# A fused attention and MLP kernel: MLP units three steps later, longer DVE sums, copies of q on ScalarE

## The chip, the cores and the metric

The kernel runs on one core of a Trainium2 chip. The metric is the device time of one execution in microseconds, as the median of several runs. PE is TensorE (PEld its weight loads), DVE is VectorE, ACT is ScalarE, POOL is GpSimd, SP is SyncE, which here only issues DMAs.

## The reference

Causal attention with a forgetting decay, for 8 batches of 8 heads, 576 positions and head dimension 64, feeds a two-layer MLP over the 4608 tokens (512 features, 2048 hidden):

```python
scores = scale * q @ k.T                       # per batch and head
cum = np.cumsum(np.log(np.clip(f, 1e-4, 1)))
scores = where(causal, -1e9, scores + cum[:, None] - cum[None, :])
attn = softmax(scores)
x = (attn @ v) rearranged to [B * S, H * D]
h = x @ w_in
g = h - np.tanh(h)
out = g @ w_out
```

The MLP needs all 8 heads of a token, so it runs behind the attention.

## The kernel before, in words

**Attention.** Heads are taken in pairs: 4 pairs per batch, 32 pairs `(b, c)` in all. `scores` (line 256) makes one of 7 tiles of a pair's transposed scores on PE (the tiles have one or two matmuls, line 266), takes the exponential on ACT (line 272) and masks on POOL (line 280). The decay is folded into three extra rows of `QT` and `KT`. `values` (line 283) multiplies with v and a column of ones (line 290), and DVE normalizes into `xn` (lines 294 to 296). `turn` (line 299) brings `xn` transposed into `XR`, a ring of four batches: for the first batch by PE, from the second by two DMA transposes on SP's queue (lines 310 and 312).

The transposed q and k come in two ways. Up to batch 2, `trans` (line 229) transposes a pair's q or k on PE into a PSUM tile, and two copies of 64 x 576 bring it to `QT` or `KT`, on DVE (line 244) or ACT (line 242). From batch 3 on, `turn_block` (line 97) does it by DMA into `TQ` and `TK`, and `place` copies on DVE (line 102). The loads of q, k and v from HBM go through POOL's queue (lines 88 to 114).

**MLP.** The 4608 tokens are 9 units of 512. `mlp1` (line 314) has 16 steps per unit: 4 matmuls of 512 columns into a PSUM tile `hps` (line 324), a tanh of -h on ACT (line 327) and an add on DVE into `gq` (line 331). `mlp2` (line 346) has 14 steps of 8 matmuls of 256 columns (line 353). It uses a Strassen-like scheme with 7 products instead of 8: `wout` is seen as 2 x 2 blocks B11 to B22, and line 205 makes the differences W1, W2, W4 and a new B12 once, 8 instructions of 128 x 1024. The unit's g is seen as blocks A11 to A22, and line 338 makes sums S1, S2 and S3 (S3 in the place of A21); line 375 makes S4 in the place of A12. `STEPS` (line 344) names the order of the products. The results are added up on DVE (`plus`, line 359; one copy on ACT, line 369) and leave by four DMAs of 256 KB per unit (line 365).

In the kernel before, `gq` holds a quarter of a unit, four steps of `mlp1`; the sums are made after every fourth step, in pieces of 512.

**The order of the work.** The order on PE, POOL, SP and DVE is the order of the program, written out by hand; on ACT a scheduler decides. The outer loop (line 424) runs over slots `p` from 0 to 32. Slot `p` holds the scores of pair `p`, the values of pair `p - 1` (behind tile 2), the transposes of pair `p + 1`, a `turn`, and the loads that `LOADS` lists for `(p, tile)`. Between these items it strews MLP steps evenly:

```python
    TAKE = (0, 0, 0, 0, 2, 8, 7, 7, 6)
            take = TAKE[p] if p < len(TAKE) else 8 - (p - len(TAKE)) % 2
```

`TAKE` gives 30 steps to slots 4 to 8, which is one unit; from slot 9 on slots take 8 and 7 by turns, 30 in four slots. So unit `u` begins with slot `4u + 5`. The last pair of batch `u`, pair `4u + 3`, has its values in slot `4u + 4`, behind tile 2, and its `turn` behind tile 3. Unit `u` reads tokens `512u` to `512u + 511`, and from unit 1 on these reach into batch `u`. What is left after slot 32 runs alone at the end (line 442): 60 steps, the last two units.

Buffers: `ps_m` has 4 PSUM tiles that `hps`, the products of `mlp2` and the tiles of `trans` share in turn; `ps_sc` has 2 for scores. `gq` has 5 buffers, `sq` (S1 and S2) 4, `th` and `ost` 2 each.

Of the kernel before, what the change touches and what calls it, by code (L numbers as in the profile page):

```python
# [21 lines left out]
def kernel(  # L22
# [10 lines left out]
    nc = tc.nc  # L33
    P = 128
# [6 lines left out]
    NPAIR = H // 2  # L41
# [5 lines left out]
    NK = NFT // 2  # L47
    HU = 256
    HE = DM // 2
    NCH = DM // P  # L50
    UW = 512
# [4 lines left out]
    wpl = ctx.enter_context(tc.tile_pool(name="wpl", bufs=1))  # L56
    aex = ctx.enter_context(tc.tile_pool(name="aex", bufs=10))
    fin = ctx.enter_context(tc.tile_pool(name="fin", bufs=3))
    gtp = ctx.enter_context(tc.tile_pool(name="gtp", bufs=5))
    tmp = ctx.enter_context(tc.tile_pool(name="tmp", bufs=2))  # L60
    acc = ctx.enter_context(tc.tile_pool(name="acc", bufs=1))
    PSUM = bass.MemoryType.PSUM
# [6 lines left out]
    W1 = wpl.tile([P, NK, HE], FP16)  # L69
    W2 = wpl.tile([P, NK, HE], FP16)  # L70
    W4 = wpl.tile([P, NK, HE], FP16)
    B11, B12 = wout[:, 0:NK, 0:HE], wout[:, 0:NK, HE:DM]
    B21, B22 = wout[:, NK:NFT, 0:HE], wout[:, NK:NFT, HE:DM]
# [114 lines left out]
    def load_wout(t0, t1):  # L188
# [3 lines left out]
    LOADS = {(0, 1): [lambda: load_qk(qn, q, 1, 0, 2), lambda: load_qk(kn, k, 1, 0, 2)],  # L192
             (0, 4): [lambda: load_qk(qn, q, 1, 2, H)],
             (1, 0): [lambda: load_qk(kn, k, 1, 2, H)],
             (1, 2): [lambda: load_win(0, DFF // 2)],
             (1, 5): [lambda: load_v_rest(1), lambda: load_v_head(1, 0)],
             (2, 1): [lambda: load_v_head(1, 1), lambda: load_win(DFF // 2, DFF)],
             (4, 0): [lambda: load_wout(0, NFT // 2)],
             (4, 2): [lambda: load_wout(NFT // 2, NFT)]}
    for n in range(NJ - 1):  # L200
        LOADS.setdefault((3, n), []).append(lambda n=n: load_v_block(1, n, 2, H))
    for n in range(2):
        ks = slice(n * NK // 2, (n + 1) * NK // 2)
        for i, (o, x, y) in enumerate(((W1, B12, B11), (B12, B22, B12), (W2, B22, W1), (W4, B21, W2))):
            LOADS.setdefault((NPAIR + 2, i), []).append(lambda o=o, x=x, y=y, ks=ks: nc.vector.tensor_tensor(
                out=o[:, ks, :], in0=x[:, ks, :], in1=y[:, ks, :], op=ALU.subtract))
    LOADS.setdefault((NPAIR, 5), []).append(lambda: load_qk(qn, q, 2, 0, H))
    LOADS.setdefault((NPAIR, 6), []).append(lambda: load_qk(kn, k, 2, 0, H))
# [18 lines left out]
    E, XN, GQ, SQ, M2 = {}, {}, {}, {}, {}  # L227
# [86 lines left out]
    def mlp1(u, s):  # L314
        pr, half = divmod(s, 2)
        ft = half * NK + pr
        hps = ps_m.tile([P, UW], FP32, tag="m", name="hps")
        t0 = u * UW % RING
        parts = [(0, t0, min(UW, RING - t0))]
        if t0 + UW > RING:  # L320
            parts.append((RING - t0, 0, t0 + UW - RING))
        for o, t, n in parts:
            for ci in range(NCH):
                nc.tensor.matmul(out=hps[:, o:o + n], lhsT=win[:, ci, ft * P:(ft + 1) * P],  # L324
                                 rhs=XR[:, ci, t:t + n], start=(ci == 0), stop=(ci == NCH - 1))
        th = tmp.tile([P, UW], FP32, tag="th", name="th")
        nc.scalar.activation(out=th, in_=hps, func=AF.Tanh, scale=-1.0)  # L327
        if s % 4 == 0:
            GQ[(u, s // 4)] = gtp.tile([P, 2, 2, UW], FP16, tag="gq", name="gq")
        gq = GQ[(u, s // 4)]  # L330
        nc.vector.tensor_tensor(out=gq[:, half, pr % 2, :], in0=hps, in1=th, op=ALU.add)  # L331
        if s % 4 == 3:
            sq = SQ[(u, s // 4)] = gtp.tile([P, 2, 2, HU], FP16, tag="sq", name="sq", bufs=4)
            a11, a21 = gq[:, 0, :, 0:HU], gq[:, 0, :, HU:UW]
            a22 = gq[:, 1, :, HU:UW]
            for o, x, y, op in ((sq[:, 0], a21, a22, ALU.add), (sq[:, 1], sq[:, 0], a11, ALU.subtract),
                                (a21, a11, a21, ALU.subtract)):
                nc.vector.tensor_tensor(out=o, in0=x, in1=y, op=op)  # L338

    LHS = {"A11": lambda u, i: GQ[(u, i)][:, 0, :, 0:HU], "A12": lambda u, i: GQ[(u, i)][:, 1, :, 0:HU],  # L340
           "A22": lambda u, i: GQ[(u, i)][:, 1, :, HU:UW], "S3": lambda u, i: GQ[(u, i)][:, 0, :, HU:UW],
           "S1": lambda u, i: SQ[(u, i)][:, 0], "S2": lambda u, i: SQ[(u, i)][:, 1]}
    LHS["S4"] = LHS["A12"]
    STEPS = [("A11", B11), ("S2", W2), ("A12", B21), ("S3", B12), ("S1", W1), ("A22", W4), ("S4", B22)]

    def mlp2(u, s):
        n, m = divmod(s, 2)
        lhs, rhs = STEPS[n]
        if m == 0:
            M2["ps"] = ps_m.tile([P, 2, HE], FP32, tag="m", name="ops")  # L350
        ps = M2["ps"]
        for kt in range(NK):
            nc.tensor.matmul(out=ps[:, m, :], lhsT=LHS[lhs](u, kt // 2)[:, kt % 2, m * P:(m + 1) * P],  # L353
                             rhs=rhs[:, kt, :], start=(kt == 0), stop=(kt == NK - 1))
        if m == 0:
            return

        def plus(src, to):
            nc.vector.tensor_tensor(out=to, in0=ps, in1=src, op=ALU.add)  # L359
            return to  # L360

        def total(src, r, e):
            ost = plus(src, tmp.tile([P, 2, HE], FP32, tag="ost", name="ost"))
            r0 = u * UW + r * HU
            nc.sync.dma_start(out=out[r0:r0 + HU, e * HE:(e + 1) * HE].rearrange("(m p) e -> p m e", p=P), in_=ost)

        if lhs == "A11":
            M2["m1"] = acc.tile([P, 2, HE], FP32, tag="m1", name="m1")
            nc.scalar.activation(out=M2["m1"], in_=ps, func=AF.Copy)
        elif lhs == "S2":  # L370
            M2["u2"] = plus(M2["m1"], acc.tile([P, 2, HE], FP32, tag="u2", name="u2"))
        elif lhs == "A12":
            total(M2["m1"], 0, 0)
            for i in range(4):
                nc.vector.tensor_tensor(out=LHS["S4"](u, i), in0=LHS["A12"](u, i), in1=LHS["S2"](u, i), op=ALU.subtract)  # L375
        elif lhs == "S3":
            M2["u3"] = plus(M2["u2"], acc.tile([P, 2, HE], FP32, tag="u3", name="u3"))
        elif lhs == "S1":
            total(M2["u3"], 1, 1)
            plus(M2["u2"], M2["u2"])  # L380
        elif lhs == "A22":
            total(M2["u3"], 1, 0)
        else:
            total(M2["u2"], 0, 1)
# [3 lines left out]
    def att_items(p):  # L388
        def put(fn, *args):
            items.append((lambda: fn(*args), True))  # L390

        items = []
        here = pairs[p] if p < len(pairs) else None
        before = pairs[p - 1] if 0 < p <= len(pairs) else None
        after = pairs[p + 1] if p + 1 < len(pairs) else None
        early = p < NPAIR
        if p == 0:
            put(trans, *here, qn, QT, "AA")
            put(trans, *here, kn, KT, "VV")
        for ti in range(len(TILES)):  # L400
            if here:
                put(scores, *here, ti)
            for load in LOADS.get((p, ti), ()):
                items.append((load, False))
            if ti == 0 and after and after[0] < FAR:
                put(trans, *after, qn, QT, "VV")
            if ti == (1 if early else 3) and after and after[0] < FAR:
                put(trans, *after, kn, KT, "VV")
            if ti == 2 and before:
                put(values, *before)  # L410
            if p < NPAIR:
                if ti == 1 and p > 1:
                    put(turn, *pairs[p - 2])
            elif p == NPAIR and ti in (1, 5):
                put(turn, *pairs[p - 2 + (ti == 5)])
            elif p > NPAIR and ti == 3:
                put(turn, *before)
        return items

    mlp = [(fn, u, s) for u in range(NU) for fn, n in ((mlp1, NFT), (mlp2, 2 * len(STEPS))) for s in range(n)]  # L420
    TAKE = (0, 0, 0, 0, 2, 8, 7, 7, 6)
    at = 0
    with tc.manual_schedule(engines={PE, mybir.EngineType.Pool, mybir.EngineType.SP, mybir.EngineType.DVE}):
        for p in range(len(pairs) + 1):
# [47 lines left out]
```

## Time and profile before

| What | us |
|---|---|
| Median of 3 runs | 394.73 |
| Lowest and highest run | 390.86, 394.89 |
| The profiled execution | 392.38 |
| Its span, first to last instruction | 390.7 |
| PE busy | 344.6 |
| DVE busy | 295.9 |
| ACT busy | 206.9 |
| POOL busy | 166.9 |

A row of the groups of instructions has the line, engine, operation, out<-in with shapes and count, then the busy time, the mean in ns, and the engine's idle time just before them with what ended it. A row of the timeline has start, length, engine, line and operation, a count where neighbours are merged, and in brackets the idle time before it and what ended it. Matmul starts are exact; their ends are modelled, so neighbours overlap. A row of the waits has the engine and line that waited, what for, the sum, how many times, and the longest. A row of the stretches has the stretch, its length, the busy time of each engine with the count, the granted TensorE clock as a share of full speed, the DMA share and GB/s.

### The profile page before, as it was taken

The numbers are of one execution on the slowest core, as the hardware profiler recorded it, in microseconds if no ns is written. First come the engines' busy times: TensorE is split into PE (matmuls) and PEld (weight loads), VectorE is DVE, ScalarE is ACT, GpSimd is POOL, SyncE is SP. The second block draws the span as 40 slices with busy tenths as digits, with TensorE's granted clock in tenths as the row PEclk, the third lists the DMA queues.
The fourth block names the chain that finished last, engine by engine and source line by source line (L and its number), as shares of the span: only waits on it lengthen the run. The fifth ranks groups of instructions, "written<-read, shape, count | busy, mean of one in ns | idle before, by whom it ended". The sixth has DMA issues, their size and how long they took to land. (4 is left out here: it accounts for less than half of the span.)

```text
span 390.7 us, 8437 instructions
## 1 busy us (share of the span) xinstructions
PE 344.6 (88%) x3156; PEld 235.0 (60%) x3156; DVE 295.9 (76%) x563; ACT 206.9 (53%) x388; POOL 166.9 (43%) x340
## 2 busy tenths in 40 slices
PE   1898977988989799969998899969999999999995
PEld 0665533864548446844587788735686577467474
DVE  7678998775999378936886588728896866876973
ACT  5588653434763478426853585427646861641620
POOL 7979622573346543754277336734222221000000
PEclk9999995998999899998999899969999999999999
DMA  8999991999939992999599969998122012103003
GB/s 102 167 183 194 207 171 18 81 142 130 108 32 100 172 142 50 92 155 147 86 69 135 175 91 64 132 151 109 33 59 82 15 30 72 55 2 107 2 1 107
DMA packets 145324, 38.79 MB, mean 99 GB/s; under 512 B 128084, under 2 KB 144196, under 8 KB 145284
## 3 DMA queue, kind: packets, MB, share of 16 engines
q0 software_dynamic: 92416, 18.37, 56.4%
q1 hardware_dynamic: 52868, 19.90, 24.5%
q8 instruction: 24, 0.39, 0.4%
q14 instruction: 16, 0.13, 0.1%
HBM read 36.85 MB, written 9.44 MB: 118 GB/s over the span
## 5 line engine op out<-in xcount | busy, mean ns | idle before, releaser
L324 PE MATMUL hps<-XR,win 128*128 128x512 f16 (+1 forms) x640 | 150.7, 373 | 21.7 <-DMA XR<-xn 16.6
L272 ACT ACTIVATE e<-ps 128x512 f16<-128x512 f32 x192 | 110.8, 598 | 51.4 <-PE ps L266 49.1
L327 ACT ACTIVATE th<-hps 128x512 f32<-128x512 f32 x144 | 86.1, 599 | 85.3 <-PE hps L324 67.3
L331 DVE TENSOR_TENSOR gq<-hps,th 128x512 f16<-128x512 f32 x144 | 96.1, 687 | 44.7 <-ACT th L327 42.2
L280 POOL TENSOR_SCALAR_AFFINE_SELECT e<-e 128x128 f16<-128x128 f16 (+1 forms) x192 | 68.3, 360 | 111.6 <-ACT e L272 109.1
L324 PEld LDWEIGHTS <-win 128*128 128x128 f16 x640 | 60.7, 101 | 60.7 <-issue 14.1
L266 PE MATMUL ps<-QT,KT 67*128 67x64 f16 (+4 forms) x384 | 81.6, 295 | 9.2 <-DMA KT<-clo 3.3
L353 PEld LDWEIGHTS <-gq 128*128 128x128 f16 x720 | 68.3, 98 | 18.2 <-DVE gq L331 4.3
L353 PE MATMUL ops<-wout,gq 128*128 128x256 f16 x576 | 75.1, 276 | 3.8 <-DVE gq L331 3.7
L266 PEld LDWEIGHTS <-KT 67*128 67x128 f16 x384 | 38.0, 103 | 48.7 <-issue 23.9
L290 PEld LDWEIGHTS <-e 128*128 128x128 f16 x896 | 34.6, 101 | 4.5 <-issue 0.8
L290 PE MATMUL av<-vn,e 128*128 128x65 f16 x896 | 35.7, 197 | 0.6 <-POOL e L280 0.6
L353 PE MATMUL ops<-W,sq 128*128 128x256 f16 x288 | 36.1, 273 | 0.0
L359 DVE TENSOR_TENSOR ost<-ops,u 128x512 f32<-128x512 f32 x27 | 18.6, 690 | 22.1 <-DMA out_dram<-ost 12.5
L113 POOL DMA_DIRECT2D vn<-in_v_dram x32 | 27.9, 874 | 3.6 <-issue 3.0
L353 PEld LDWEIGHTS <-sq 128*128 128x128 f16 x288 | 26.9, 98 | 3.8
L296 DVE TENSOR_TENSOR xn<-av,rs 128x640 f16<-128x640 f32 x32 | 26.4, 825 | 1.1
L280 POOL TENSOR_SCALAR_AFFINE_SELECT el<-el 128x128 f16<-128x128 f16 x32 | 9.8, 306 | 33.7 <-ACT el L272 33.7
L244 DVE COPY QT<-t 64x576 f16<-64x576 f16 x22 | 17.6, 802 | 7.5 <-PE t L235 7.4
L94 POOL DMA_DIRECT2D kn<-in_k_dram x25 | 21.2, 848 | 2.3 <-issue 2.3
L94 POOL DMA_DIRECT2D qn<-in_q_dram x25 | 21.2, 847 | 2.1 <-issue 1.8
L272 ACT ACTIVATE el<-ps 128x128 f16<-128x128 f32 x32 | 8.8, 275 | 24.3 <-PE ps L266 24.2
(58 smaller groups left out, 248.2 us busy)
## 6 DMA issues: line engine op xcount, KB each, us to landing
out_dram<-ost SPq DMA_DIRECT2D x36, 256.0 KB
vn<-in_v_dram POOLq DMA_DIRECT2D x24, 128.0 KB, 4.4
qn<-in_q_dram POOLq DMA_DIRECT2D x20, 128.0 KB, 3.6
kn<-in_k_dram POOLq DMA_DIRECT2D x20, 128.0 KB, 5.0
win<-in_moe_w_in_dram POOLq DMA_DIRECT2D x2, 1024.0 KB, 11.5
wout<-in_moe_w_out_dram POOLq DMA_DIRECT2D x2, 1024.0 KB, 12.0
XR<-xn SPq DMA_TRANSPOSE x56
vn<-in_v_dram POOLq DMA_DIRECT2D x12, 64.0 KB, 4.1
```

Of the source, the lines that this page charges most:

```text
L94: nc.gpsimd.dma_start(out=dst[b % 2][0:pn, n, :].rearrange("p (h d) -> p h d", h=H), in_=src[b, :, n * P:n * P + pn, :].rearrange("h p d - ...
L113: nc.gpsimd.dma_start(out=vn[b % 2][:, n, h0:h1, 0:D], in_=v[b, h0:h1, n * P:(n + 1) * P, :].rearrange("h p d -> p h d"))
L266: nc.tensor.matmul(out=ps[:, col:col + n], lhsT=KT[b % 2][:, h, j * P:(j + 1) * P], rhs=QT[b % 2][:, h, i0:i0 + n])
L272: nc.scalar.activation(out=e[:, lo:hi], in_=ps[:, lo:hi], func=AF.Exp, scale=qscale)
L280: nc.gpsimd.affine_select(out=view, in_=view, compare_op=ALU.is_ge, fill=0.0, base=0, pattern=pat, channel_multiplier=-1)
L290: nc.tensor.matmul(out=av[:, a, ib, :], lhsT=E.pop((b, c, a, j, ib)), rhs=vn[b % 2][:, j, 2 * c + a, 0:D + 1], start=(j == 0), stop=(j == ib))
L296: nc.vector.tensor_tensor(out=xn.rearrange("p i (a d) -> p a i d", a=2), in0=av[:, :, :, 0:D], in1=rs.to_broadcast([P, 2, NJ, D]), op=ALU. ...
L324: nc.tensor.matmul(out=hps[:, o:o + n], lhsT=win[:, ci, ft * P:(ft + 1) * P], rhs=XR[:, ci, t:t + n], start=(ci == 0), stop=(ci == NCH - 1))
L327: nc.scalar.activation(out=th, in_=hps, func=AF.Tanh, scale=-1.0)
L331: nc.vector.tensor_tensor(out=gq[:, half, pr % 2, :], in0=hps, in1=th, op=ALU.add)
L353: nc.tensor.matmul(out=ps[:, m, :], lhsT=LHS[lhs](u, kt // 2)[:, kt % 2, m * P:(m + 1) * P], rhs=rhs[:, kt, :], start=(kt == 0), stop=(kt ...
L359: nc.vector.tensor_tensor(out=to, in0=ps, in1=src, op=ALU.add)
```

## The change

- `TAKE` gives 2, 7, 6, 6 and 6 steps to slots 4 to 8, 27 instead of 30. Every unit now begins three steps into slot `4u + 5`, and 63 steps are left after slot 32.
- `gq` and `sq` hold half a unit (8 steps); the sums are made after every eighth step in pieces of 1024, and so is S4. Both have 2 buffers. The SBUF that they take goes from 28 to 24 KB per partition.
- The eight weight differences move from slot 6 to slots 5 (W1 behind tiles 3 and 4, B12 behind tiles 5 and 6) and 6 (W2 behind tiles 1 and 2, W4 behind tiles 4 and 5).
- In `STEPS` the product of A12 comes second and that of S2 third.
- The copies of the transposed q are on ACT for slots 4 to 10; those of k stay on DVE.
- `ost` has 3 buffers instead of 2.

```diff
-    gtp = ctx.enter_context(tc.tile_pool(name="gtp", bufs=5))
+    gtp = ctx.enter_context(tc.tile_pool(name="gtp", bufs=2))
...
-            LOADS.setdefault((NPAIR + 2, i), []).append(lambda o=o, x=x, y=y, ks=ks: nc.vector.tensor_tensor(
+            LOADS.setdefault((NPAIR + 1 + i // 2, (3, 5, 1, 4)[i] + n), []).append(lambda o=o, x=x, y=y, ks=ks: nc.vector.tensor_tensor(
                 out=o[:, ks, :], in0=x[:, ks, :], in1=y[:, ks, :], op=ALU.subtract))
...
-        if s % 4 == 0:
-            GQ[(u, s // 4)] = gtp.tile([P, 2, 2, UW], FP16, tag="gq", name="gq")
-        gq = GQ[(u, s // 4)]
-        nc.vector.tensor_tensor(out=gq[:, half, pr % 2, :], in0=hps, in1=th, op=ALU.add)
-        if s % 4 == 3:
-            sq = SQ[(u, s // 4)] = gtp.tile([P, 2, 2, HU], FP16, tag="sq", name="sq", bufs=4)
+        if s % 8 == 0:
+            GQ[(u, s // 8)] = gtp.tile([P, 2, NK // 2, UW], FP16, tag="gq", name="gq")
+        gq = GQ[(u, s // 8)]
+        nc.vector.tensor_tensor(out=gq[:, half, pr % 4, :], in0=hps, in1=th, op=ALU.add)
+        if s % 8 == 7:
+            sq = SQ[(u, s // 8)] = gtp.tile([P, 2, NK // 2, HU], FP16, tag="sq", name="sq")
...
-    STEPS = [("A11", B11), ("S2", W2), ("A12", B21), ("S3", B12), ("S1", W1), ("A22", W4), ("S4", B22)]
+    STEPS = [("A11", B11), ("A12", B21), ("S2", W2), ("S3", B12), ("S1", W1), ("A22", W4), ("S4", B22)]
...
-            ost = plus(src, tmp.tile([P, 2, HE], FP32, tag="ost", name="ost"))
+            ost = plus(src, tmp.tile([P, 2, HE], FP32, tag="ost", name="ost", bufs=3))
...
-            for i in range(4):
+            for i in range(2):
                 nc.vector.tensor_tensor(out=LHS["S4"](u, i), in0=LHS["A12"](u, i), in1=LHS["S2"](u, i), op=ALU.subtract)
...
-                put(trans, *after, qn, QT, "VV")
+                put(trans, *after, qn, QT, "VV" if early else "AA")
...
-    TAKE = (0, 0, 0, 0, 2, 8, 7, 7, 6)
+    TAKE = (0, 0, 0, 0, 2, 7, 6, 6, 6)
```

The reads in `mlp2` change their indices with the halves (`kt // 4`, `kt % 4`).

More of the change, by code (lines that the diff above doesn't have):

```diff
@@ L327, in mlp1 @@
         nc.scalar.activation(out=th, in_=hps, func=AF.Tanh, scale=-1.0)
-        if s % 4 == 0:
-            GQ[(u, s // 4)] = gtp.tile([P, 2, 2, UW], FP16, tag="gq", name="gq")
-        gq = GQ[(u, s // 4)]
-        nc.vector.tensor_tensor(out=gq[:, half, pr % 2, :], in0=hps, in1=th, op=ALU.add)
-        if s % 4 == 3:
-            sq = SQ[(u, s // 4)] = gtp.tile([P, 2, 2, HU], FP16, tag="sq", name="sq", bufs=4)
-            a11, a21 = gq[:, 0, :, 0:HU], gq[:, 0, :, HU:UW]
-            a22 = gq[:, 1, :, HU:UW]
+        if s % 8 == 0:
[4 more added lines that the diff above has]
+            sq = SQ[(u, s // 8)] = gtp.tile([P, 2, NK // 2, HU], FP16, tag="sq", name="sq")
+            a11, a21, a22 = gq[:, 0, :, 0:HU], gq[:, 0, :, HU:UW], gq[:, 1, :, HU:UW]
             for o, x, y, op in ((sq[:, 0], a21, a22, ALU.add), (sq[:, 1], sq[:, 0], a11, ALU.subtract),
@@ L352, in mlp2 @@
         for kt in range(NK):
-            nc.tensor.matmul(out=ps[:, m, :], lhsT=LHS[lhs](u, kt // 2)[:, kt % 2, m * P:(m + 1) * P],
+            nc.tensor.matmul(out=ps[:, m, :], lhsT=LHS[lhs](u, kt // 4)[:, kt % 4, m * P:(m + 1) * P],
                              rhs=rhs[:, kt, :], start=(kt == 0), stop=(kt == NK - 1))
```

## The prediction, made before the changed kernel ran

> **What bounds the kernel now.** I read the page first, then the waits of PE, then a table of stretches cut at the slots' first score matmuls, then the timeline around the long waits. A "slot" is one pass of the loop over `p`.
>
> ```profile
> span 390.7 us, 8437 instructions
> PE 344.6 (88%) x3156; PEld 235.0 (60%) x3156; DVE 295.9 (76%) x563; ACT 206.9 (53%) x388; POOL 166.9 (43%) x340
> ```
> ```profile
> PE hps L324 <- DMA XR<-xn: 16.6, 5, 4.1
> PE hps L324 <- DVE gq L331: 5.0, 8, 2.0
> ```
>
> PE is busy 88% of the span. Its largest wait is 16.6 us in five pieces, for the transposes that bring an attention output into XR. In the stretches below the columns are length, then busy time of PE, PEld, DVE, ACT and POOL, then the granted TensorE clock, DMA share and GB/s.
>
> ```profile
> 37.89:48.73 10.84, 10.07 (x88) 5.45 (x86) 9.83 (x18) 7.58 (x15) 7.17 (x12) 1.00 1.26 207
> 48.73:66.38 17.65, 12.07 (x88) 6.23 (x87) 17.19 (x31) 7.29 (x14) 3.53 (x8) 0.80 0.99 105
> 76.89:85.01 8.12, 8.12 (x104) 6.88 (x102) 7.43 (x13) 3.53 (x7) 6.42 (x14) 1.00 1.23 144
> 85.01:100.69 15.68, 11.79 (x88) 5.98 (x87) 9.39 (x17) 7.57 (x15) 7.02 (x14) 0.89 1.29 139
> 100.69:112.38 11.69, 9.49 (x82) 5.12 (x83) 11.05 (x21) 7.76 (x15) 3.22 (x9) 1.00 0.41 70
> 130.35:144.32 13.97, 11.20 (x76) 5.41 (x75) 7.37 (x14) 7.44 (x15) 6.51 (x12) 0.88 1.48 156
> 170.63:185.71 15.08, 11.20 (x76) 5.43 (x75) 7.36 (x14) 7.43 (x15) 6.38 (x12) 0.89 1.41 148
> 212.03:226.31 14.28, 11.26 (x108) 8.84 (x107) 7.36 (x14) 7.43 (x15) 6.75 (x13) 0.88 1.52 167
> 252.66:269.53 16.87, 12.54 (x76) 6.31 (x75) 7.56 (x14) 7.43 (x15) 6.37 (x12) 0.80 1.27 134
> 295.84:305.48 9.64, 9.37 (x76) 4.91 (x75) 7.35 (x14) 7.37 (x15) 2.13 (x7) 1.00 0.26 74
> ```
>
> Rows one to four are slots 5, 6, 8 and 9. Row five is slot 10. The last five are slots 13, 17, 21, 25 and 29, which hold the same PE work: the start of a new MLP unit. Slot 29 takes 9.64 us at full clock without a wait; the other four take 4.33, 5.44, 4.64 and 7.23 us more. The timeline says why, and the clock says that a wait costs twice.
>
> ```profile
> 133.87 0.38 PE L324 MATMUL hps<-XR,win 128*128 128x512 f16 x1 [2.49 <-DMA XR<-xn]
> 215.97 0.27 PE L324 MATMUL hps<-XR,win 128*128 128x256 f16 x1 [2.80 <-DMA XR<-xn]
> 257.75 0.59 PE L324 MATMUL hps<-XR,win 128*128 128x512 f16 x1 [4.06 <-DMA XR<-xn]
> ```
> ```profile
> 59.30:69.50 10.20, 8.05 (x35) 4.37 (x35) 8.34 (x16) 3.85 (x7) 2.93 (x5) 0.50 0.08 16
> 90.00:93.40 3.40, 3.40 (x16) 1.52 (x14) 2.65 (x4) 1.68 (x3) 0.03 (x1) 0.50 0.94 146
> 134.40:137.80 3.40, 3.40 (x12) 1.36 (x10) 1.38 (x2) 2.05 (x4) 1.58 (x3) 0.51 1.53 135
> 216.30:219.70 3.40, 3.40 (x18) 2.36 (x17) 1.38 (x2) 2.15 (x4) 1.46 (x3) 0.50 1.80 138
> 257.20:264.00 6.80, 6.25 (x42) 3.44 (x42) 2.08 (x3) 2.77 (x5) 2.46 (x4) 0.50 1.23 182
> ```
>
> After each of the five waits PE runs at half clock: four times for 3.4 us (three of the four are shown, two of them after the waits of 2.49 and 2.80) and once for 6.8 us. Half of that time is lost: (4 x 3.4 + 6.8) / 2 = 10.2 us. So the five waits cost 16.6 + 10.2 = 26.8 us. A sixth half-clock stretch, 10.2 us from 59.3, follows waits for DVE in slot 6.
>
> **Unit starts, three steps later.** Nothing is added; three MLP steps now stand ahead of the old place, with the attention work that lies between steps. How much PE time that is can be read in slot 29, where nothing waits: the first step starts at 296.06, the fourth at 300.00.
>
> ```profile
> 296.06 1.03 PE L324 MATMUL hps<-XR,win 128*128 128x512 f16 x4
> ...
> 300.00 1.03 PE L324 MATMUL hps<-XR,win 128*128 128x512 f16 x4
> ```
>
> The cover is 3.94 us. The waits run from 2.49 (unit 2) to 4.06 (unit 5), so at most 0.12 us stays, in unit 5, provided that XR lands when it does now. What sets the landing: the two transposes leave SP as soon as xn is written, and DVE writes xn after the values.
>
> ```profile
> 249.56 0.38 SPq L365 DMA_DIRECT2D out_dram<-ost  x1
> 250.84 1.23 SPq L310 DMA_TRANSPOSE XR<-xn  x1
> 252.14 1.22 SPq L312 DMA_TRANSPOSE XR<-xn  x1
> ```
>
> Landing comes 257.75 - 250.84 = 6.9 us after the first issue. In the changed order the output DMA at 249.56 comes behind these two on SP, and the four small sums of line 375 that DVE did just ahead of this xn fall in the slot before. Both can only bring XR forward. The two outputs that end a unit now follow the five transposes into TQ on SP; a third `ost` buffer keeps DVE from waiting for them. POOL keeps its order. I take 26.7 us of gain; the bounds are 0 (XR moves along with the unit) and 26.8.
>
> The Trainium skill, "TensorE: Matmul & The Clock Gate", section "HAM oscillation — how this bites in real kernels", gives an abstract rule of "no PE-idle gaps >~3.4µs". By it the waits of 2.49 and 2.80 would not have halved the clock, the clock's part would be (2 x 3.4 + 6.8) / 2 = 6.8 instead of 10.2, and my sum would end 3.4 us higher. The trace does not agree: the rows at 134.40 and 216.30 show half clock after shorter waits, so I give that no chance here.
>
> **DVE: sums in pieces of 1024, copies moved, differences spread.**
>
> ```profile
> L338 DVE TENSOR_TENSOR gq<-gq 128x512 f16<-128x512 f16 x36 | 16.9, 471 | 0.0
> L338 DVE TENSOR_TENSOR sq<-gq 128x512 f16<-128x512 f16 x36 | 15.6, 433 | 1.2
> L338 DVE TENSOR_TENSOR sq<-sq,gq 128x512 f16<-128x512 f16 x36 | 15.5, 430 | 1.2
> L244 DVE COPY QT<-t 64x576 f16<-64x576 f16 x22 | 17.6, 802 | 7.5 <-PE t L235 7.4
> ```
> ```profile
> L205 DVE TENSOR_TENSOR W<-wout x2: 681/684/686, 52.6 to 53.2; 128x1024 f16<-128x1024 f16 x2
> ```
> ```profile
> L242 ACT ACTIVATE QT<-t x2: 796/800/805, 7.2 to 8.0; 64x576 f16<-64x576 f16 x2
> ```
>
> Before: 108 sums of 512, 48.0 us. After: 54 of 1024, at the 0.684 us of line 205, 36.9 us. So 11.1 us less on DVE, but a burst is 2.05 us instead of 1.3. The q copies of seven slots (4 to 10) leave DVE, 2 x 0.80 us each, and load ACT by as much. All of this counts only where DVE is late.
>
> That is slots 5 and 6 first: DVE is busy 9.83 + 17.19 = 27.0 of 28.5 us. From it go two pairs of q copies (3.2), one gq (14 steps become 13, 0.7), and three bursts of 1.3 become one of 2.05 (1.9). The eight differences stay in these two slots. 21.2 us are left. PE needs 10.07 - 0.87 = 9.2 and 8.12 (slot 8's length, six steps and no wait), 17.3 us, so DVE still sets these slots, at 21.2. Slots 7 and 8 hold six steps each, 2 x 8.12. With one half-clock stretch of 3.4 us (1.7; the bounds are none and today's 5.1) it makes 39.1 instead of 85.01 - 37.89 = 47.1: 8.0 us of gain. Of this 2.6 us (3 x 0.87) is work that comes back at the end, where slot 32 leaves 63 steps instead of 60.
>
> The new place of the differences adds a wait. They read wout, whose halves must have landed.
>
> ```profile
> L189 POOL DMA_DIRECT2D wout<-in_moe_w_out_dram x2: 883/887/891, 33.7 to 35.2; - x2
> DMA to landing us min/median/max: 10.2/12.0/13.9
> ```
>
> The halves land at 33.7 + 10.2 = 43.9 and 35.2 + 13.9 = 49.1 at the latest. The first difference stands behind six gq (at about 43 to 44), the first that reads the second half behind nine gq, two KT copies and the first burst (at about 49 to 50). I take 0; if DVE came 2 us sooner it would hold gq, KT copies and xn behind it, and PE through the PSUM buffers, for 2 us.
>
> Slot 10 waited for DVE too:
>
> ```profile
> 107.14 1.89 PE L324 MATMUL hps<-XR,win 128*128 128x512 f16 x8 [0.31 <-DVE gq L331]
> 112.38 0.39 PE L266 MATMUL ps<-QT,KT 67*128 67x512 f16 x1 [1.62 <-DVE KT L244]
> ```
>
> With 1.6 us of q copies off DVE these 1.9 us go. What is late next there is ACT: 7.76 + 1.6 = 9.4 of a slot of 9.8 us. The copies' cost on ACT lies between 0 and 7 x 1.6 = 11.2 us; ACT has 3 us or more to spare in each of these slots today, so I take 0.5 in all.
>
> **The larger bursts elsewhere.** A burst holds gq, and so PSUM buffers, 0.75 us longer. Fourteen bursts lie in the slots, so the bounds are 0 and 10.5 us. PE waited 5.0 us for gq in the whole run, so I take 1.5, mainly in slots 11, 15, 19, 23 and 27, where the place copies now stand among the last gq.
>
> **The tail.** Two units run there alone, and DVE sets the pace of their first halves:
>
> ```profile
> 341.23 2.69 DVE L331 TENSOR_TENSOR gq<-hps,th 128x512 f16<-128x512 f32 x4
> 345.09 2.69 DVE L331 TENSOR_TENSOR gq<-hps,th 128x512 f16<-128x512 f32 x4
> ```
>
> Four steps take 3.86 us there against 3.47 on PE. Now the first eight go at PE's 0.87, then the burst, then seven gq at 0.67 until A11 can end: 1.7 + 7 x 0.87 + 0.7 + 2.05 + 4.7 = 15.2 us against 15.9. I take 0.7 per unit, 1.4 in all. A12 before S2 gives DVE the 1.7 us of A12 to finish its sums, so S2 does not wait.
>
> **The sum.** -26.7 (XR and its clock) - 8.0 (slots 5 to 8) - 1.9 (slot 10) + 2.6 (three steps at the end) - 1.4 (tail) + 1.5 (bursts) + 0.5 (ACT) = -33.4. The profiled execution took 392.38 us, 1.7 more than its span; that gives 359.0. The median of the runs, 394.73, lies 2.35 above that execution; I leave that to the range.
>
> **Rivals.**
> One: XR lands later as well. Today POOL sends the slot's second load of v only when the wait is over, since its selects follow the scores; with PE running on, one or two 128 KB loads go out while the transposes are under way. If that delays them by 2 us, 16.6 + 5 x 2 - 5 x 3.94 = 6.9 us of waits stay, and if the clock falls as today, 10.2 more: about 376. The Trainium skill, "DMA: Bandwidth & Descriptors", section "Queues, rings and completion order", speaks for it: each DMA engine takes turns between the queues that have work. Against it: most of the 6.9 us passes before the second load could go.
> Two: the first units gain nothing but their three steps, because DVE meets wout too early or the clock stays low: 8.0 - 2.6 = 5.4 more, 364.4. DVE is the bound there in either case, which speaks for it.
> Three, the other side: the 2.05 us bursts find DVE so late that all PSUM buffers are full, and PE stands for the burst and then runs at half clock. Fourteen times (2.05 + 1.7) is 52 us, which outweighs 33.4: about 411. It decides from about 9 of the 14 on. Against it: DVE is busy 7.4 of 9.64 us in a slot without waits.
>
> **How the numbers follow.** My forecast has 0.68, rival one 0.14, rival two 0.13, rival three 0.03, no change for a reason that I don't see 0.02. The range reaches from 351 (no half clock early, no new waits, XR early) to 370, past rival two and half-way to rival one, and leaves out 0.2. About 1% is what a measurement of this kernel can tell from no change. Faster 0.95, within 1% 0.02, slower 0.03.
>
> **What would show it.** In the new profile the waits for XR should be under 1 us in sum, with PEclk at 1.00 from slot 9 on; slots 13, 17, 21, 25 should take 9.6 to 10 us; the sums should be 54 of about 0.68 us; slot 9 should start near 77. It is wrong if XR waits remain with half clock behind them, if waits for gq exceed some 8 us, or if DVE shows a wait for wout.

## The result and the profile after

The changed kernel takes 370.6 us, the median of four runs (369.06 to 373.72); the kernel before, in four runs beside it, takes 393.7. The ratio is 0.943, with a 95% interval of 0.935 to 0.952: faster by 23.1 us, where 33.4 had been forecast, and 0.6 us above the upper end of the predicted range. The profiled execution took 373.72 us, 3.1 above the median. Ratios here and below leave out the runs that came out slower than the others of the same kernel, medians do not: of the four runs of e8 one, of 369.30 us, is such a run, and the median of the other three is 364.5.

The page of the changed kernel, its span and busy times, and then its longest waits of PE that are not the start of the program:

```profile
span 371.6 us, 8348 instructions
PE 337.5 (91%) x3156; PEld 232.4 (63%) x3156; DVE 280.7 (76%) x477; ACT 215.6 (58%) x402; POOL 164.8 (44%) x340
```
```profile
PE ops L352 <- DVE gq L331: 7.0, 10, 1.0
...
PE hps L324 <- DVE gq L331: 3.9, 4, 2.5
```

No wait for XR is left. At the top now stands a wait of `ops`, the first product of `mlp2`, for `gq`: ten times, 0.7 us on average, all in slots 11, 15, 19, 23 and 27. The kernel before had this wait too, but its six lay in slot 6 and behind the last slot:

```profile
PE ops L353 <- DVE gq L331: 3.7, 6, 1.9
```

The stretches, cut at the first score matmul of slots 5, 6, 9, 10, 13 and 15 (columns as in the prediction):

```profile
42.42:52.59 10.17, 9.33 (x84) 5.00 (x82) 6.61 (x12) 8.65 (x16) 6.41 (x12) 1.00 1.25 200
52.59:64.86 12.27, 8.62 (x78) 4.60 (x79) 12.09 (x21) 8.91 (x17) 3.41 (x10) 1.00 1.65 110
82.75:92.53 9.78, 9.78 (x101) 6.58 (x98) 6.62 (x12) 7.43 (x13) 6.51 (x13) 1.00 2.23 161
92.53:105.29 12.76, 10.13 (x84) 5.34 (x82) 9.46 (x16) 8.56 (x16) 3.02 (x9) 0.92 0.87 133
125.12:134.38 9.26, 9.26 (x89) 6.06 (x88) 5.34 (x10) 5.87 (x12) 6.29 (x12) 1.00 1.82 148
142.71:154.48 11.77, 9.90 (x93) 6.28 (x91) 10.93 (x20) 6.96 (x14) 6.51 (x13) 1.00 0.93 86
```

And slot 15 of the kernel before, which the prediction did not show:

```profile
152.68:162.23 9.55, 9.43 (x105) 7.62 (x102) 8.47 (x17) 5.22 (x10) 6.60 (x12) 1.00 0.89 58
```

Read the two slots 15 together. PE's work goes from 9.43 to 9.90, but the slot from 9.55 to 11.77, and DVE is busy 10.93 of it. It is the same in slots 11, 19, 23 and 27. Laid side by side, the two profiles give this account of the change in time, against the terms of the prediction's sum (lengths in us, from the starts of the slots' first score matmuls):

| Stretch | Before | After | Change | Forecast |
|---|---|---|---|---|
| up to slot 4 | 31.3 | 33.8 | +2.5 | 0 |
| slot 4 | 6.55 | 8.62 | +2.1 | part of the +0.5 for ACT |
| slots 5 to 8 | 47.1 | 40.3 | -6.8 | -8.0 |
| slot 9 | 15.7 | 9.8 | -5.9 | with the next |
| slots 13, 17, 21, 25 | 60.2 | 37.1 | -23.1 | -26.7 with slot 9 |
| slot 10 | 11.7 | 12.8 | +1.1 | -1.9, and part of the +0.5 for ACT |
| slots 11, 15, 19, 23, 27 | 47.7 | 57.5 | +9.8 | +1.5 |
| slot 29 to the end | 94.8 | 96.4 | +1.6 | +2.6 - 1.4 |

From slot 5 on the sum is 352.8 before and 329.2 after, 23.6 less (the slots that the table leaves out change by 0.1 in sum), which is near what the medians show.

The first line is not the change's. Slot 4 begins between 29.8 and 34.1 us in the fourteen traced kernels, and two of the experiments (e4, e11), which are the same program as the kernel before up to slot 5, begin it at 33.6 and 33.2. What differs is the pace of PE in the slots ahead of it. The changed kernel and e3, from 20 us to the start of slot 4:

```profile
20.00:33.80 13.80, 12.90 (x124) 8.93 (x122) 10.25 (x18) 10.09 (x20) 10.53 (x24) 1.00 1.23 189
20.00:29.88 9.88, 8.38 (x122) 5.95 (x122) 8.94 (x16) 9.27 (x20) 9.23 (x21) 1.00 1.27 183
```

124 matmuls are busy for 12.90 us in the one and 122 for 8.38 us in the other. The clock column says 1.00 for both, so it does not show this.

The second line is the change's, in these two profiles. In slot 4 the copies of q on ACT stand ahead of exponentials that PE needs, and half clock follows (slot 4 of the kernel before, then a matmul and a stretch in slot 4 of the changed kernel):

```profile
31.34:37.89 6.55, 5.87 (x73) 3.70 (x72) 5.35 (x10) 5.60 (x11) 6.25 (x15) 1.00 1.63 189
```
```profile
37.07 0.22 PE L266 MATMUL ps<-QT,KT 67*128 67x64 f16 x2 [0.86 <-ACT e L272]
```
```profile
38.40:41.80 3.40, 3.40 (x16) 1.77 (x15) 0.89 (x2) 2.35 (x5) 2.54 (x6) 0.51 1.21 171
```

With these copies on DVE slot 4 takes 6.55 us in the kernel before and 6.29 in e4 and e11; with the copies on ACT it takes 7.74 to 8.63 in the eight traced kernels that have them there. Other things lengthen this slot too: e3, e8 and e9, with the copies on DVE, take 7.74 to 8.97 us, e3 and e9 with a wait for `win` of 0.8 and 1.4 us, e8 with slow matmuls. In what follows the profiled executions are compared from slot 5 on.

What bounds slot 15 is seen in its order on DVE, and in the two matmuls that wait (first DVE, then PE):

```profile
147.24 0.67 DVE L331 TENSOR_TENSOR gq<-hps,th 128x512 f16<-128x512 f32 x1
147.94 1.43 DVE L102 COPY QT<-TQ 64x1152 f16<-64x1152 f16 x2
149.41 0.69 DVE L331 TENSOR_TENSOR gq<-hps,th 128x512 f16<-128x512 f32 x1
150.01 1.19 DVE L102 COPY KT<-TK 64x1152 f16<-64x1152 f16 x2
...
151.56 0.82 DVE L296 TENSOR_TENSOR xn<-av,rs 128x640 f16<-128x640 f32 x1
152.30 0.68 DVE L331 TENSOR_TENSOR gq<-hps,th 128x512 f16<-128x512 f32 x1
153.02 0.69 DVE L337 TENSOR_TENSOR sq<-gq 128x1024 f16<-128x1024 f16 x1
```
```profile
150.15 1.16 PE L352 MATMUL ops<-wout,gq 128*128 128x256 f16 x9 [0.98 <-DVE gq L331]
...
153.04 0.28 PE L352 MATMUL ops<-wout,gq 128*128 128x256 f16 x1 [0.75 <-DVE gq L331]
```

DVE has no pause here. The unit's last `gq` instructions stand between place copies and an `xn`, and the product of A11 reads them as soon as they are there, at 150.15 and 153.04. In the kernel before, the unit's last `gq` of this slot is ahead of the short burst and of all place copies (DVE in slot 15):

```profile
155.01 0.69 DVE L331 TENSOR_TENSOR gq<-hps,th 128x512 f16<-128x512 f32 x1 [0.78 <-ACT th L327]
...
157.09 2.26 DVE L102 COPY QT<-TQ 64x1152 f16<-64x1152 f16 x4
```

### The profile page after: what moved, and what is told of

It reads as the page before. It is cut to its first block, busy times and chain, and to the rows that moved or that the text cites. A ratio compares the mean times of both kernels' runs of the same rounds, so it can differ in the third digit from the quotient of the medians.

```text
span 371.6 us, 8348 instructions
## 1 busy us (share of the span) xinstructions
PE 337.5 (91%) x3156; PEld 232.4 (63%) x3156; DVE 280.7 (76%) x477; ACT 215.6 (58%) x402; POOL 164.8 (44%) x340
## 3 DMA queue, kind: packets, MB, share of 16 engines
q1 hardware_dynamic: 52868, 19.90, 26.7%
## 4 chain that ended last, share of the span: by engine, by line
PE 55%; DVE 25%; ACT 9%; issue 6%; DMA 3%; POOL 1%; POOLq 0%; DVEq 0%; SPq 0%; ACTq 0%
PE ops L352 26%; PE hps L324 13%; PE ps L266 9%; DVE gq L331 8%; ACT e L272 4%; PE av L290 4%; ACT th L327 4%; DVE QT L102 3%; DVE sq L337 3%; DVE xn L296 3%; DVE KT L244 2%; PE t L235 2%; DMA XR<-xn 2%; DVE KT L102 1%; DVE gq L337 1%
## 5 line engine op out<-in xcount | busy, mean ns | idle before, releaser
L324 PE MATMUL hps<-XR,win 128*128 128x512 f16 (+1 forms) x640 | 144.0, 362 | 5.1 <-DVE gq L331 3.9
L327 ACT ACTIVATE th<-hps 128x512 f32<-128x512 f32 x144 | 87.0, 606 | 66.1 <-PE hps L324 54.4
L331 DVE TENSOR_TENSOR gq<-hps,th 128x512 f16<-128x512 f32 x144 | 97.7, 688 | 34.2 <-ACT th L327 32.7
L280 POOL TENSOR_SCALAR_AFFINE_SELECT e<-e 128x128 f16<-128x128 f16 (+1 forms) x192 | 67.0, 352 | 100.8 <-ACT e L272 98.9
L324 PEld LDWEIGHTS <-win 128*128 128x128 f16 x640 | 58.6, 98 | 55.9 <-issue 10.2
L266 PE MATMUL ps<-QT,KT 67*128 67x64 f16 (+4 forms) x384 | 80.0, 295 | 11.5 <-DMA KT<-clo 4.6
L358 DVE TENSOR_TENSOR ost<-ops,u 128x512 f32<-128x512 f32 x27 | 18.7, 691 | 28.1 <-PE ops L352 28.0
L352 PEld LDWEIGHTS <-sq 128*128 128x128 f16 x288 | 27.1, 97 | 4.8
L94 POOL DMA_DIRECT2D qn<-in_q_dram x25 | 21.2, 846 | 2.6 <-issue 2.6
L244 DVE COPY KT<-t 64x576 f16<-64x576 f16 x24 | 19.1, 797 | 0.3
L352 PE MATMUL ops<-W,gq 128*128 128x256 f16 x144 | 18.2, 272 | 0.0
```

The source lines that it names most:

```text
L94: nc.gpsimd.dma_start(out=dst[b % 2][0:pn, n, :].rearrange("p (h d) -> p h d", h=H), in_=src[b, :, n * P:n * P + pn, :].rearrange("h p d - ...
L244: nc.vector.tensor_copy(out=to, in_=of)
L266: nc.tensor.matmul(out=ps[:, col:col + n], lhsT=KT[b % 2][:, h, j * P:(j + 1) * P], rhs=QT[b % 2][:, h, i0:i0 + n])
L280: nc.gpsimd.affine_select(out=view, in_=view, compare_op=ALU.is_ge, fill=0.0, base=0, pattern=pat, channel_multiplier=-1)
L331: nc.vector.tensor_tensor(out=gq[:, half, pr % 4, :], in0=hps, in1=th, op=ALU.add)
L352: nc.tensor.matmul(out=ps[:, m, :], lhsT=LHS[lhs](u, kt // 4)[:, kt % 4, m * P:(m + 1) * P], rhs=rhs[:, kt, :], start=(kt == 0), stop=(kt ...
```

## The experiments

Twelve kernels were run, each timed against the kernel before; all compute the whole reference. Ratios are given with their 95% intervals, and the changed kernel's own is 0.943 [0.935, 0.952].

**e1: the place copies moved away from the last gq.** Two copies of q go behind tiles 5 and 6 of slot 4u + 5, two of k behind tiles 5 and 6 of slot 4u + 7.

```diff
-                    LOADS.setdefault((p0 + 3, 2 * n + a), []).append(...)
+                    LOADS.setdefault((p0 + 1 + 2 * n, 5 + a), []).append(...)
```

> The changed kernel with the eight place copies per batch moved: those of q from tiles 0 and 1 of slot 4u+7 to tiles 5 and 6 of slot 4u+5, those of k from tiles 2 and 3 of slot 4u+7 to its tiles 5 and 6. Theory P (the copies among the last four gq make A11 and A12 wait in slots 11, 15, 19, 23, 27): the 1.9 us of PE waits in each of these slots go, the slots fall from 11.8 to about 9.9 us, and the time falls by 6 to 8 us, to about 363. Theory B (the burst of 1024 sums makes them wait): the waits stay, the time moves by less than 2 us.

Measured: 386.78 us, 0.987 [0.982, 0.993], so slower than the changed kernel. Its waits of PE:

```profile
PE ps L266 <- DVE KT L102: 12.0, 5, 2.4
PE hps L324 <- DVE gq L331: 9.0, 10, 2.5
...
PE ops L352 <- DVE gq L331: 0.2, 1, 0.2
```

The wait in question goes from 7.0 to 0.2 us, so the copies did stand in the way. But the copies of k, behind the burst and at the slot's end, are late for the first scores of the next slot (12.0 us in five waits), and slot 15 grows to 13.1 us, although the copies of q have left it: they run at 136.84 in slot 14. (DVE is still busy 11.59 us in slot 15, since the longer slot takes in sums that came behind it before.) So it is not the amount of DVE work alone that counts; what stands last in the slot counts too.

**e2: the sums back in pieces of 512.**

```diff
-        if s % 8 == 7:
-            sq = SQ[(u, s // 8)] = gtp.tile([P, 2, NK // 2, HU], FP16, tag="sq", name="sq")
+        if s % 4 == 3:
+            sq = SQ[(u, s // 4)] = gtp.tile([P, 2, 2, HU], FP16, tag="sq", name="sq", bufs=4)
```

(with `gq`, the indices of its reads, the four instructions of S4 and the 5 buffers as before)

> The changed kernel with the sums back in pieces of 512, after every fourth step, with the buffers of before. Theory B: waits for gq in slots 15, 19, 23, 27 fall by more than half, time about 366. Theory P: DVE has more work in just those slots, so the waits grow, and the first units and the tail lose what the larger pieces gave: about 374 to 378.

Measured: 369.83 us, 0.944 [0.938, 0.950]: no difference. The stretch of slot 15, and the wait:

```profile
139.62:151.02 11.40, 9.75 (x92) 6.28 (x91) 10.89 (x23) 6.72 (x14) 6.84 (x13) 1.00 0.96 89
```
```profile
PE ops L352 <- DVE gq L331: 9.0, 14, 1.5
```

With the short burst the slot still takes 11.40 us with DVE busy 10.89, so the length of the burst is not what makes it long. The five slots 11, 15, 19, 23 and 27 lose 1.3 us in sum, and slots 5 to 8 take 41.28 us instead of 40.33.

**e3: the copies of q back on DVE.**

```diff
-                put(trans, *after, qn, QT, "VV" if early else "AA")
+                put(trans, *after, qn, QT, "VV")
```

> The changed kernel with the copies of transposed q of slots 4 to 10 back on DVE. As predicted (DVE is late in slots 5, 6 and 10, ACT is not): 3.2 us more in slots 5 and 6, 1.5 to 2 more in slot 10, about 375. Rival (the copies on ACT delay the exponentials and the tanh behind them, which is why slots 4 and 10 came out 2 and 3 us longer than forecast): slots 4 and 10 shorten by 2 to 4 us together, time 368 to 371.

Measured: 367.8 us, 0.938 [0.935, 0.942]; the interval overlaps the changed kernel's. By the profiles slots 5 to 8 become 1.2 us longer (41.50 for 40.33), slot 10 1.4 shorter (11.38 for 12.76), slot 11 another 0.6 and slot 4 0.9 (7.74 for 8.62, with a wait of 0.8 us for `win` in it). What the copies do on ACT in slot 10 of the changed kernel, on ACT, DVE and PE:

```profile
94.78 1.65 ACT L242 ACTIVATE QT<-t 64x576 f16<-64x576 f16 x2
96.45 0.60 ACT L327 ACTIVATE th<-hps 128x512 f32<-128x512 f32 x1
```
```profile
97.08 0.69 DVE L331 TENSOR_TENSOR gq<-hps,th 128x512 f16<-128x512 f32 x1 [1.43 <-ACT th L327]
```
```profile
103.24 1.84 PE L324 MATMUL hps<-XR,win 128*128 128x512 f16 x4 [2.49 <-DVE gq L331]
```
```profile
103.30:106.70 3.40, 3.40 (x10) 1.37 (x10) 2.67 (x4) 1.62 (x4) 0.41 (x1) 0.50 0.23 43
```

The copies hold a tanh for up to 1.65 us, DVE stands idle for 1.43 us and then has its burst and `xn` ahead of later `gq`; PE waits 2.49 us for a free PSUM buffer and runs at half clock for 3.4 us behind it.

**e4: the kernel before with only the new TAKE.**

```diff
-    TAKE = (0, 0, 0, 0, 2, 8, 7, 7, 6)
+    TAKE = (0, 0, 0, 0, 2, 7, 6, 6, 6)
```

> The kernel before with the new TAKE alone. As predicted: the XR waits (16.6 us) and the half clock behind them (10.2 us) go, slots 5 to 8 shrink by the 2.6 us of three steps that come back at the end, so about 394 - 26.8 = 367 without the other parts, plus the waits behind the place copies by theory P (5 x 1.9 = 9), 376. Rival: without the lighter DVE the XR transposes are issued later and some of the XR waits remain, over 380.

Measured: 380.23 us, 0.971 [0.965, 0.976]. The waits for XR are gone here too. Slot 15:

```profile
145.45:157.88 12.43, 9.75 (x93) 6.29 (x92) 11.49 (x24) 6.72 (x14) 6.86 (x13) 1.00 0.97 89
```

So the three steps alone, without any other part of the change, fill this slot with DVE work. They are worth 12.1 us by the medians of this comparison (392.34 to 380.23); the rest of the change's 23.1 us, some 11, comes from its other parts. One of them is seen in this kernel's longest wait of PE behind the start:

```profile
PE ops L353 <- DVE sq L338: 8.3, 5, 1.8
```

It is the product of S2 that waits for its sum, once in each of slots 11, 15, 19, 23 and 27. Neither the changed kernel nor e2 has this wait, and in e2, which also has the short burst, these five slots take 56.2 us where e4 takes 61.4. The product of A12 ahead of S2 is what fits; no run tests it alone. The prediction had named this effect for the program's end, and no gain in these slots.

**e5: the place copies of q on POOL.** They stand in slot 4u + 6, behind tiles 2 and 4.

```diff
-        nc.vector.tensor_copy(out=dst[b % 2]...
+        (nc.gpsimd if dst is QT else nc.vector).tensor_copy(out=dst[b % 2]...
...
-                    LOADS.setdefault((p0 + 3, 2 * n + a), []).append(...)
+                    LOADS.setdefault((p0 + 2 + n, 2 + 2 * a if n == 0 else 2 + a), []).append(...)
```

> The changed kernel with the place copies of q on POOL, in slot 4u+6 behind tiles 2 and 4, where POOL is busy 2.6 of 8.3 us; those of k stay on DVE in slot 4u+7. Theory D (DVE's sum of work bounds slots 15, 19, 23: 12.0 us of 11.8): 2.2 us leave DVE there, slots 11, 15, 19, 23 and 27 fall by 1.5 to 1.9 us each, 364 to 366. Rival G (the gq wait for something else, or POOL's selects come late behind copies): the slots stay at 11.4 us or more, or new PE waits for POOL or for the copies come up in their place, 368 to 376.

Measured: 369.53 us, 0.943 [0.934, 0.951]: no difference in all. Slot 15:

```profile
140.83:151.71 10.88, 9.72 (x93) 6.35 (x91) 9.53 (x17) 6.96 (x14) 8.63 (x14) 1.00 0.97 90
```

With 1.4 us less on DVE the slot is 0.9 us shorter (10.88 for 11.77), as it should be if DVE bounds it. But slot 10 took 13.76 us, 1.0 more, with waits for `gq` of up to 3.5 us.

**e6: two steps later instead of three.** All else as in the changed kernel.

```diff
-    TAKE = (0, 0, 0, 0, 2, 7, 6, 6, 6)
+    TAKE = (0, 0, 0, 0, 2, 7, 7, 6, 6)
```

> The changed kernel with units two steps later instead of three (TAKE 2, 7, 7, 6, 6). Cover by slot 29 of the kernel before: 298.23 - 296.06 = 2.17 us. If XR lands as before, waits of 1.4, 0.3, 1.4, 0.6 and 1.9 us are left, 5.7 in sum, for five at most; with the output DMA no longer ahead of the transposes they may be 0.5 to 1 us shorter each. If waits of 1 to 2 us also bring half clock, it costs up to 5 x 1.7 more. 371 to 378; if XR lands earlier than I think, no waits and a time as of the changed kernel or 2 us below it, since one gq less falls into slots 15, 19, 23, 27.

Measured: 363.09 us, 0.928 [0.920, 0.936]: 7.5 us below the changed kernel by the medians and 6.1 by the ratios (0.943 - 0.928 of 393.7); from slot 5 on its profile has 323.3 us where the changed kernel's has 329.2. The two intervals just touch; that of e12, with the same order, lies clear of the changed kernel's. Its slots 13 and 15, and its wait for XR:

```profile
119.05:129.59 10.54, 9.42 (x85) 5.69 (x84) 6.04 (x11) 6.46 (x13) 6.32 (x12) 1.00 2.24 148
137.92:147.79 9.87, 9.41 (x97) 6.84 (x96) 8.90 (x15) 6.67 (x13) 6.50 (x12) 1.00 1.03 90
```
```profile
PE hps L324 <- DMA XR<-xn: 3.8, 4, 1.3
```

Slot 15 falls by 1.9 us and slot 13 grows by 1.3. Three waits for XR of 1.1 to 1.3 us and one of 0.3 come back, but the clock in slot 13 stays at 1.00. The next lines say why slot 15 is so much lighter: the groups of `gq` in slot 15 of the kernel before, of the changed kernel, and of this one.

```profile
L331 DVE TENSOR_TENSOR gq<-hps,th 128x512 f16<-128x512 f32 x4 | 2.7, 684 | 0.9 <-ACT th L327 0.8
```
```profile
L331 DVE TENSOR_TENSOR gq<-hps,th 128x512 f16<-128x512 f32 x8 | 5.4, 685 | 0.7 <-ACT th L327 0.6
```
```profile
L331 DVE TENSOR_TENSOR gq<-hps,th 128x512 f16<-128x512 f32 x6 | 4.1, 686 | 0.9 <-ACT th L327 0.8
```

Four with no delay, eight with three steps, six with two; with one step (e10) there are four again. The second and third step of delay put two `gq` of 0.69 us each into this slot.

**e7: the eight differences back in slot 6.**

```diff
-            LOADS.setdefault((NPAIR + 1 + i // 2, (3, 5, 1, 4)[i] + n), []).append(...)
+            LOADS.setdefault((NPAIR + 2, i), []).append(...)
```

> The changed kernel with the eight weight differences back in slot 6. As predicted (DVE's sum over slots 5 and 6 counts, not their place): within 2 us of the changed kernel. Rival (slot 6 alone is bound, 2.7 us more of DVE in it, with longer waits for the copies of k and half clock): slots 5 to 8 longer by 2.5 to 5 us, 373 to 376.

Measured: 372.39 us, 0.952 [0.944, 0.961]; not told apart from the changed kernel by the intervals. By the profiles slots 5 to 8 take 42.96 us instead of 40.33, with 4.6 us of waits for KT. So the spreading is worth some 2 us by these profiles; the prediction had named no gain for it.

**e8: e5 and e3 together.** Their two edits in one kernel.

> Both: place copies of q on POOL, and the trans copies of q on DVE throughout. If the gains add up: 367.8 - 5 = 361 to 364. Rival G: 366 or more.

Measured: 366.26 us, 0.933 [0.923, 0.943], not told apart from e5 or from e3 by the intervals. Slot 10 falls from e5's 13.76 to 11.86 and slots 5 to 8 rise from 40.34 to 41.42. That is about what e3 did alone. Slot 11 falls too, from 11.32 to 9.25 us.

**e9: e6 and e3 together.** Their two edits in one kernel.

> Units two steps later and the copies of transposed q on DVE throughout, else the changed kernel. If the two gains add up (363.1, and some 2 to 3 us as from 370.6 to 367.8): 360.5 to 362. If the copies on DVE then collide with the gq that slot 12 and slot 8 now hold (DVE 8.9 of 8.4 us there): 363 to 365.

Measured: 367.87 us, 0.935 [0.931, 0.940]; every run is slower than every run of e6, though the intervals of the ratios overlap. Slots 7 and 8 of e9 with the wait between them:

```profile
62.54:74.79 12.25, 8.39 (x102) 6.82 (x103) 12.02 (x19) 5.04 (x10) 7.23 (x13) 0.97 0.91 83
74.79:86.50 11.71, 11.21 (x102) 8.46 (x102) 6.88 (x12) 3.45 (x7) 5.70 (x11) 0.73 0.71 51
```
```profile
74.79 0.61 PE L266 MATMUL ps<-QT,KT 67*128 67x512 f16 x1 [3.69 <-DVE KT L244]
```

With two steps, slot 6 holds one step more than with three; with the copies of q on DVE as well, DVE is busy 12.02 of 12.25 us in slot 7, the copies of k come 3.69 us late, and slot 8 runs at a mean clock of 0.73. Slots 5 to 8 take 47.7 us, where e6 takes 41.1. So with two steps the copies on ACT earn their place in these slots, and in slot 10 they cost nothing: it takes 11.33 us in e6 and 11.46 in e9. The 1.4 us of e3 are a cost of the copies beside three steps.

**e10: one step later.**

```diff
-    TAKE = (0, 0, 0, 0, 2, 7, 6, 6, 6)
+    TAKE = (0, 0, 0, 0, 2, 7, 7, 7, 6)
```

> Units one step later (TAKE 2, 7, 7, 7, 6), else the changed kernel. Cover 1.08 us instead of 2.17, so waits for XR of 2.2, 2.2, 2.2 and about 1.4 us, 8 in sum, against 3.8 with two later. If a wait of 2.2 us still brings half clock (as 2.49 did before, and 1.1 with two later did not): about four stretches of 3.4 us, 1.7 us each, time 363 + 4 + 7 = 372 to 376. If it does not: 366 to 369.

Measured: 377.09 us, 0.962 [0.955, 0.969]. Its wait for XR, one of the five, and the clock behind it:

```profile
PE hps L324 <- DMA XR<-xn: 12.1, 5, 3.2
```
```profile
164.11 0.38 PE L324 MATMUL hps<-XR,win 128*128 128x512 f16 x1 [2.18 <-DMA XR<-xn]
```
```profile
164.80:168.20 3.40, 3.40 (x36) 2.31 (x35) 1.70 (x4) 1.40 (x3) 1.29 (x2) 0.51 1.79 149
```

One step is not enough: waits of 1.57 to 3.23 us stay. Slots 15, 19, 23 and 27 show no wait for DVE (slot 15 takes 9.26 us).

**e11: the kernel before with only TAKE of e6.**

```diff
-    TAKE = (0, 0, 0, 0, 2, 8, 7, 7, 6)
+    TAKE = (0, 0, 0, 0, 2, 7, 7, 6, 6)
```

> The kernel before with TAKE 2, 7, 7, 6, 6 alone. Theory D (three later was dear because DVE's work of slots 15, 19, 23, 27 exceeds the slot): with two later the slots 4u+7 take about 10 us instead of 12.4, and 380.2 falls to 371 to 374; what is left to 363 is the early slots. Rival: with the sums of 512 the slots stay over 12 us, 378 or more.

Measured: 371.11 us, 0.943 [0.938, 0.948]. Two numbers changed in the kernel before bring as much as the whole change. Slot 15 takes 10.10 us, with DVE busy 9.80, where three steps (e4) give 12.43.

**e12: e6 with the sums in pieces of 512.** The edits of e6 and e2 together.

> Units two steps later with the sums back in pieces of 512, else the changed kernel. If the larger pieces are worth little, as with three later (369.8 against 370.6): 362 to 365. By the prediction's account (11 us of DVE work, 1.4 us of the tail, 1.9 in slots 5 and 6) it should lose 3 or more: 366 to 369.

Measured: 363.39 us, 0.924 [0.919, 0.929], the same as e6. So the larger pieces bring nothing that can be measured, with two steps as with three. By the profiles they gain 2.1 us in slots 5 to 8 (41.1 for 43.2) and cost 1.7 in slots 11, 15, 19, 23 and 27 (48.7 for 47.0).

## Why the prediction was wrong

**XR and its clock (forecast -26.7): right.** The waits are gone, and no half clock follows them; slots 13, 17, 21 and 25 take 9.26 to 9.29 us. Of the 29.0 us by which slots 9, 13, 17, 21 and 25 became shorter, 0.38 us per slot is PE work that now lies in slot 4u + 7 (slot 29, which never waited, goes from 9.64 to 9.26); without those five times 0.38, 27.1 us remain. How much cover it takes is seen in e6, e10 and e4: two steps nearly cover the transposes, one does not, three do so without the rest of the change. Rival one, a later landing, did not come.

**Three steps later ("Nothing is added"): this is the step that failed.** The prediction counted what the three steps cover on PE and what they cost at the program's end. It put at nothing what they do to DVE in slots 11, 15, 19, 23 and 27 (slots 4u + 7), and gave those slots +1.5 us for the larger bursts alone. They lost 9.8 us, or 7.9 without the PE work that moved there. The sum of these five slots, by how many steps later the units begin:

| Steps later | Sums of 512, old order of products | Sums of 512, new order | Sums of 1024, new order |
|---|---|---|---|
| 0 | 47.7 (before) | | |
| 1 | | | 46.3 (e10) |
| 2 | 50.2 (e11) | 47.0 (e12) | 48.7 (e6) |
| 3 | 61.4 (e4) | 56.2 (e2) | 57.5 (changed) |

The old order has the product of S2 second, the new one that of A12; the new order's kernels also have the rest of the change. Down each column the third step costs 8.8 to 11.2 us. Across, the larger burst costs 1.3 to 1.7 us, which is the size that the prediction gave it; since it had taken this size and not worked it out, that is partly luck. What the steps add is DVE work. Those that leave slot 4u + 5 put their `gq` instructions beside the place copies, the last burst, `xn` and the first result of `mlp2`. DVE in slot 15 is busy 8.01 us with one step (e10), 8.90 with two (e6) and 10.93 with three, and the slot takes 9.26, 9.87 and 11.77; so the third step costs 1.9 us there and saves 1.3 in slot 13. In e5 1.4 us less of DVE work made the slot 0.9 us shorter. How much is the amount of this work and how much its order is not separated: e1 had fewer copies in the slot and lost more.

The prediction had summed up DVE per slot for slots 5 and 6 only, and had taken the rest from the 5.0 us that PE waited for `gq` in the old order, where 4 `gq` lay in slot 15. That reading also left out the 3.7 us that `ops` waited for `gq`. One of its signs of being wrong did show: waits for `gq` of more than some 8 us. They are 10.9 us in sum (7.0 and 3.9).

**Slots 5 to 8 (forecast -8.0): right in the main, -6.8.** DVE still sets slot 6 (12.09 of 12.27 us busy) but no longer slot 5 (6.61 of 10.17), so the two take 22.4 us where DVE's sum had given 21.2 and is now 18.7. One half-clock stretch of 3.4 us stays, as taken. The place of the differences, costed at 0, is worth about 2 us by e7's profile, and no wait for `wout` appeared. Rival two, in which these slots give only the 2.6 us of their three steps, did not happen.

**The copies on ACT (forecast +0.5 in all, and -1.9 in slot 10): wrong, +2.1 in slot 4 and +1.1 in slot 10.** In slot 10 the wait for KT was to go with the copies of q off DVE. In its place came the tanh behind those copies, then the burst, a wait of 2.49 us and half clock. e3 shows the copies' part by undoing that one line: 11.38 us. The room on ACT that the prediction named, 3 us or more in each slot, holds for slot 10 (7.76 us of 11.69 busy), but not for slot 4, where ACT was already busy 5.60 of 6.55 us. And in slot 10 the mean room said nothing about the 1.65 us in which a tanh must stand behind two copies.

**The tail (forecast -1.4) and the end (+2.6): right.** Unit 7, the first of the two that run alone, takes 26.86 us instead of 27.51, so 0.65 where 0.7 was forecast; with e2's sums of 512 it is 27.51 again. The three kinds of sums took, in the changed kernel:

```profile
L337 DVE TENSOR_TENSOR gq<-gq 128x1024 f16<-128x1024 f16 x18 | 13.4, 743 | 0.0
...
L337 DVE TENSOR_TENSOR sq<-gq 128x1024 f16<-128x1024 f16 x18 | 12.6, 698 | 0.6
L337 DVE TENSOR_TENSOR sq<-sq,gq 128x1024 f16<-128x1024 f16 x18 | 12.4, 692 | 0.6
```

That is 38.4 us, 1.5 more than forecast and 9.6 less than before. Off the end of the program this was worth 1.0 us (against e2) and 2.1 (e6 against e12) in slots 5 to 8, about what the longer burst cost later.

**Rival three (bursts that fill PSUM, 411 us): its mechanism showed once**, in slot 10, and not fourteen times.

In sum, the forecast missed by 8.3 us in slots 4u + 7, 2.5 in slot 10, 1.2 in slots 5 to 8 and 0.4 at the end, and by 2.3 us the other way in the slots with XR. Most of what is left of the distance from 359.0 to the profiled 373.72 is the 2.1 us of slot 4 and the 2.5 us by which slot 4 begins later in that execution.

**What stays open.** From the first issue of the two transposes to a use of XR that waited for them it takes 5.6 to 6.9 us in the kernel before, 4.8 to 6.3 in e6 and 5.2 to 6.5 in e10; the runs do not settle why. Nor do they say why the matmuls of the first slots run at their full pace sooner in some executions than in others.

## What to carry to other kernels

Moving work so that it covers a transfer moves everything that this work hands on: sum up the busy time of the other engines, here DVE, in each stretch of the new order, not only where the wait goes away. A cover need not be complete; two steps, which left waits of 1.1 us with no half clock behind them, beat three that left none, by some 6 us. And a mean of free time on an engine does not tell whether a copy put there will stand ahead of something that is waited for.

## What the runs showed of the hardware that was not expected

The half clock came after shorter waits than the prediction's rows had shown, and the length of one wait does not settle it. In e10 a wait of 2.18 us was followed by 3.4 us at 0.51 and one of 1.97 us was not. In e1, of five waits of 2.39 and 2.40 us three were followed by half clock and two were not, and in e8 one of 2.42 us was not. But 3.4 us at 0.50 also followed one of 1.69 us in e1 (slot 23), one of 1.76 in e9 (slot 6) and one of 1.21, with one of 0.27 close behind it, in e4 (slot 10), and in slot 4 of the changed kernel waits of no more than 0.86 us. In e6 no half clock followed any wait behind slot 4, the longest of them 1.41 us. The Trainium skill, "TensorE: Matmul & The Clock Gate", section "HAM oscillation — how this bites in real kernels", has as an abstract rule "no PE-idle gaps >~3.4µs"; read as leave for shorter gaps, it does not agree with these runs, nor with the wait of 2.49 us in slot 10 of the changed kernel.
